# Two staging cycles instead of one, in the first pair of blocks that two phases share

## The chip, the cores and the metric

One Trainium2 chip, one core. The metric is the device time of one execution, in microseconds (us). Engines: TensorE (PE, matrix products), VectorE (DVE), ScalarE (ACT), GpSimd (POOL, nearly idle here) and SyncE (SP, which issues almost all transfers, in order).

## The reference

```python
qn = q / (norm(q, axis=1) + 1e-6);  kn = k / (norm(k, axis=1) + 1e-6)   # over 6016 tokens
a = softmax(kn.T @ qn / tau)                   # 256 x 256
x = v @ a                                      # 6016 x 256
h = relu(x @ w_in);   x = (h * h) @ w_out      # 2048 wide
xn = x / sqrt(mean(x * x) + 1e-6) * rms_g
out = (silu(xn @ w_gate) * (xn @ w_val)) @ w_out2   # 1536 wide
```

All is float32. The kernel splits each operand into a high and a low part and makes three products of one.

## The kernel before

The 6016 tokens are twelve blocks (ten of 512, two of 448). The attention matrix is folded into `w_in`, so the first layer is one product with `m_h`/`m_l`. Blocks 0 to 3 take the plain way (`mlp1`). From pair `FIRST = 2` on (blocks 4 and 5) two blocks go through together (`mlp1_pair`): seven products of combined operands take the place of eight. A pair has eight groups; a group is seven products (21 matmuls, L1415) and four times six matmuls of the second product (L110 to L112, `acc`). The second layer (`mlp2`, L1547) comes after all pairs.

Besides its own work, a pair carries two queues of small steps for ACT and DVE, taken one step of each at three places of every group (`aside`):

- `side`: the norm of the results of the pair before, and then `pair_steps`, which forms that pair's seven operands x0, x4, x6, x3, x1, x2, x5 for the second layer. `hi(i)` casts the high part into a staging tile on ACT (L1099) and stores it (L1102); `lo(i)` makes the low part on DVE (L1110) and stores it (L1111), one step later.
- `tokens`: `v_steps`, which forms the seven v operands of the next pair in the same manner (ACT L1279, DVE L1287, one store at L1342), in the order v0, v4, v3, v1, v2, v6, v5.

All engines take their instructions in the order in which this code is written. The rows of instructions below are in that order.

In pair `FIRST` both queues draw their tiles from one cycle, `first_stage`: tile `ys`, tile `p6`, tile `ys` (the pool has two `ys` tiles), in turn, whoever asks. So that two steps do not ask at once, `aside` stops after one that stages (`staged`). In the pairs after it, the pair operands have two tiles of their own:

```python
first_stage = staged(*["ys", "p6", "ys"] * 4, "ys", "ys")
...
stage = first_stage if first else staged("ys", "p2", "ys") if last else kept(2)
```

`kept(2)` takes two `ys` tiles once and hands them out in turn. At the end of a pair, SP fetches the next pair's v operands (L1162, L1364) and loads the raw v blocks of the pair after that (L464), which DVE transposes (L1266).

Of the kernel before, what the change touches and what calls it, by code (L numbers as in the profile page):

```python
# [11 lines left out]
F32R = mybir.dt.float32r  # L12
# [8 lines left out]
P = 128  # L21
NB = 512
# [6 lines left out]
def attn_moe_kernel(ctx: ExitStack, tc, q, k, v, tau, w_in, w_out, w_gate, w_val, w2, rms_g, out):  # L29
# [16 lines left out]
    q, k, v = q[0], k[0], v[0]  # L46
# [9 lines left out]
    FIRST = NP - 4  # L56

    ctx.enter_context(tc.manual_schedule())
    wp = ctx.enter_context(tc.tile_pool(name="wp", bufs=1))
# [4 lines left out]
    def f32(t):  # L64
        return t.bitcast(F32)
# [7 lines left out]
    def acc(i):  # L73
        return ps.tile([P, NB], F32, tag=f"acc{i}", name=f"acc{i}", bufs=2)
# [44 lines left out]
    NC7 = 7  # L119
# [349 lines left out]
    def place(k, dt=F32R):  # L469
        pool = vp if k < 2 else xp  # L470
        return pool.tile([P, 2, NB], dt, tag=f"p{k}", name=f"p{k}")
# [581 lines left out]
    def staged(*tags):  # L1053

        turns = cycle(tags)

        def tile():
            t = next(turns)
            if t[0] == "p":
                return place(int(t[1]))  # L1060
            pool, k = (xp, 2) if t == "ys" else (vp, 1)
            return pool.tile([P, 2, NB], F32R, tag=t, name="xp", bufs=k)

        return tile

    def kept(count):

        turn, ts = cycle(range(count)), []

        def tile():  # L1070
            if not ts:
                ts.extend(xp.tile([P, 2, NB], F32R, tag="ys", name="xp", bufs=2) for _ in range(count))
            return ts[next(turn)]

        return tile

    def only(e, f):
        def g():
            f()

        g.only = e
        return g
# [253 lines left out]
    def through_dram(p, tile):  # L1336

        def into(i, n):
            if p not in v_dram:
                v_dram[p] = dp.tile([P, NC7, 2, NB], F32, tag=f"v{p}", name="vd")  # L1340
            t = tile()[:, :, :n]
            return t[:, 0], t[:, 1], lambda: nc.sync.dma_start(out=v_dram[p][:, i, :, :n], in_=f32(t))  # L1342

        return into
# [21 lines left out]
    def mlp1_pair(p, ops, side, after_product, after_group):  # L1366


        n = blocks[2 * p][1]
        o = {}  # L1370
        G = NF1 // 2
        if not pw:
            pw.extend(place(k, F32) for k in (3, 4, 5))
        rx, ry, sq = (x[:, :, :n] for x in pw)
        left = []

        def down(f, t, d, ph, pl, first, last):
            def g():
                if first:
                    o[t, d] = acc(d)[:, :n]  # L1380
                ds = slice(d * P, (d + 1) * P)
                mm3(o[t, d], wo_h[:, f, ds], wo_l[:, f, ds], ph, pl, first, last)
                if last:
                    nc.scalar.copy(out=pair_state(p)[:, SLOT[t][d], :n], in_=o[t, d])
                    summed[p] = summed.get(p, 0) + 1

            return g

        def square(r, q, f, t, first, last, lag):

            st = {}

            def hi():
                w = work()[:, :, :n]
                st["h"], st["l"] = w[:, 0], w[:, 1]
                nc.scalar.activation(out=st["h"], in_=r, func=AF.Square)  # L1396

            def full(act):
                if act:
                    nc.scalar.activation(out=q, in_=r, func=AF.Square)  # L1400
                else:
                    nc.vector.tensor_tensor(out=q, in0=r, in1=r, op=ALU.mult)  # L1402

            def lo():
                nc.vector.tensor_tensor(out=st["l"], in0=q, in1=f32(st["h"]), op=ALU.subtract)  # L1405
                due = slots["n"] + lag
                waiting.extend((due, down(f, t, d, st["h"], st["l"], first, last)) for d in range(KC))

            return hi, full, lo

        def group(g):
            def product(i, a, bank, start):
                xh, xl = ops[i]
                for j, (w, x) in enumerate(((0, xh), (1, xh), (0, xl))):
                    nc.tensor.matmul(bank, m_part(a, w, g), x, start=start and j == 0, stop=j == 2,  # L1415
                                     skip_group_check=not start)
                after_product(g, i)

            def aside(k=1):
                staged = False  # L1420
                for q in [side] * k + [tokens]:
                    if q and not getattr(q[0], "takes_bank", False):
                        if p == FIRST and staged and getattr(q[0], "staged", False):
                            break
                        f = q.pop(0)
                        if f is None:
                            continue
                        staged = getattr(f, "staged", False)
                        x = f()
                        if x:  # L1430
                            x()

            turn3 = slots["g"] % 3
            slots["g"] += 1
            b0, *b = [mm()[:, :n] for _ in range(4)]
            bh, bu, bv = b[turn3:] + b[:turn3]
            f0, f1, first, last = 2 * g, 2 * g + 1, g == 0, g == G - 1
            cp, sums = nc.scalar.copy, nc.vector._custom_dve
            product(0, A11, b0, True)
            old = left.pop() if left else leftover.pop() if leftover else None  # L1440
            cp(out=bu, in_=b0)
            if old:
                old[0]()
                old[1](False)
                old[2]()
            down_slot()
            product(3, S1, bh, True)
            aside()
            down_slot()
            product(1, S2, bu, False)  # L1450
            uw = work(F32)[:, :, :n]
            u, w = uw[:, 0], uw[:, 1]
            cp(out=bv, in_=bu)
            cp(out=u, in_=bu)
            down_slot()
            product(4, A12, b0, False)
            nc.scalar.activation(out=rx[:, 0], in_=b0, func=AF.Relu)  # L1457
            hi, full, lo = square(rx[:, 0], sq[:, 0], f0, 0, first, False, 3)
            hi()
            full(False)  # L1460
            lo()
            down_slot()
            product(2, S3, bv, False)
            cp(out=w, in_=bv)
            sums(TENSOR_ADD_SAT, out=rx[:, 1], in0=bh, in1=w, s0=FMAX, s1=0.0)  # L1465
            down_slot()
            down_slot()
            if side and getattr(side[0], "takes_bank", False):
                side.pop(0)(b0)()
            aside()  # L1470
            hi, full, lo = square(rx[:, 1], sq[:, 1], f1, 1, first, False, 2)
            hi()
            full(g % 2 == 0)
            lo()
            product(5, A22, bv, False)
            nc.scalar.activation(out=ry[:, 0], in_=bv, func=AF.Relu)
            hi, full, lo = square(ry[:, 0], sq[:, 0], f1, 0, False, last, 3)
            hi()
            full(True)
            down_slot()  # L1480
            product(6, S4, bh, False)
            r, q = ry[:, 1], sq[:, 1]
            if p == NP - 1 and last:
                x = work(F32)[:, :, :n]
                r, q = x[:, 0], x[:, 1]
            sums(TENSOR_ADD_SAT, out=r, in0=bh, in1=u, s0=FMAX, s1=0.0)
            lo()
            aside(1 + (p > FIRST and g == 1))
            down_slot()
            left.append(square(r, q, f0, 1, False, last, 4))  # L1490
            after_group(g)

        for g in range(G):
            group(g)
        leftover.append(left.pop())
# [278 lines left out]
    ys = {b: parts[b][2] for b in (0, 1)}  # L1774
# [147 lines left out]
    side, tokens = [], []  # L1922
    side.extend(kept_steps)
    drained.append(lambda: (side.insert(0, n0[0]), side.extend(n1 + pair_steps(FIRST - 1, first_stage))))
    first_stage = staged(*["ys", "p6", "ys"] * 4, "ys", "ys")
    for p in range(FIRST, NP):
        nxt = {}
        last = p == NP - 1
# [1 line left out]
        stage = first_stage if first else staged("ys", "p2", "ys") if last else kept(2)  # L1930
        if last:
            last_chunk["gb"] = only("dve", seq(last_chunk["va"], last_chunk["gb"]))
            last_chunk["vb"] = only("dve", seq(last_chunk["gc"], last_chunk["vb"]))
            tokens += [last_chunk.get(x) for x in LAST_CHUNK]
            side += [bridge.h, bridge.l]
        elif first:
            tokens += v_steps(p + 1, through_dram(p + 1, stage))
        else:
            tokens += wide_steps
        if p + 2 < NP:  # L1940
# [206 lines left out]
```

## Time and profile before

| | |
|---|---|
| median of 3 runs | 1116.4 us (1115.68 to 1116.91) |
| the profiled execution: time, span | 1116.82 us, 1115.0 us |
| PE busy | 1097.9 us, 98% |
| PE weight load busy | 923.7 us, 83% |
| DVE busy, ACT busy | 828.1 us (74%), 787.8 us (71%) |
| mean granted TensorE clock | 0.997 |

PE is busy nearly everywhere; of 40 slices of the span only two are below 90% (70% each): the one from 306.6 to 334.5 us and the last. Matmuls overlap, so the busy share says little of pace; the pace is read from the starts of matmuls.

### The profile page before, as it was taken

How to read it: one execution, taken by the hardware profiler on the slowest of the kernel's cores; microseconds unless marked ns; L12 is line 12 of the kernel's file. 1: busy time of each engine (PE TensorE's matmuls, PEld its weight loads, DVE VectorE, ACT ScalarE, POOL GpSimd, SP SyncE). 2: the span in 40 equal slices, each digit the busy share in tenths (PEclk: the TensorE clock that was granted, in tenths of full speed). 3: DMA queues.
4: the chain of work that ended last, by engine and by line, in shares of the span. 5: the costliest groups of instructions: out<-in, count | busy, mean ns of one | idle time of the engine just before them, and what ended most of it. 6: DMA issues, size and time to landing. Idle time of an engine off the chain costs nothing.

```text
span 1115.0 us, 14668 instructions
## 1 busy us (share of the span) xinstructions
PE 1097.9 (98%) x5122; PEld 923.7 (83%) x5122; DVE 828.1 (74%) x1305; ACT 787.8 (71%) x1441; POOL 57.8 (5%) x72
## 2 busy tenths in 40 slices
PE   9999999999979999999999999999999999999997
PEld 8978888888757888889988888888888888888997
DVE  7988888778857987988958888777556666665655
ACT  8788888787657777778777777776665556555554
POOL 2621101000000000000000000000000000000000
PEclk9999999999999999999999999999999999999999
DMA  9642222221344263271276666204423241404001
GB/s 347 211 113 96 76 57 86 71 100 57 123 170 123 94 242 92 104 259 60 87 267 254 211 222 203 97 9 164 132 76 133 76 133 45 156 20 123 19 20 34
DMA packets 115818, 138.33 MB, mean 124 GB/s; under 512 B 52000, under 2 KB 73504, under 8 KB 115616
## 3 DMA queue, kind: packets, MB, share of 16 engines
q1 hardware_dynamic: 113472, 136.54, 36.5%
q10 hardware_dynamic: 2272, 0.85, 0.3%
q8 instruction: 40, 0.66, 0.2%
q14 instruction: 34, 0.28, 0.1%
HBM read 91.10 MB, written 46.27 MB: 123 GB/s over the span
## 4 chain that ended last, share of the span: by engine, by line
PE 69%; DMA 1%; DVE 0%; SPq 0%; issue 0%; ACT 0%; DVEq 0%
PE mm L1547 30%; PE mm L1415 10%; PE acc L111 10%; PE acc L112 10%; PE acc L110 10%; DMA p<-in_v_dram 1%; PE acc L1679 0%; SPq L464 0%; SPq L1364 0%; SPq L1162 0%; DVE sh L1405 0%; DVE vx L1266 0%; DVE xp L1110 0%; DVE ot L1693 0%; DVE hp L1636 0%
## 5 line engine op out<-in xcount | busy, mean ns | idle before, releaser
L1547 PE MATMUL mm<-p,gv 128*128 128x512 f32 (+1 forms) x1188 | 301.9, 387 | 0.0
L1547 PEld LDWEIGHTS mm<-p,gv 128*128 128x128 f32 x1188 | 222.0, 188 | 44.8 <-DVE hp L1627 1.0
L1652 DVE TENSOR_TENSOR sh<-hp,sh 128x512 fp32r<-128x512 f32 (+1 forms) x144 | 97.9, 680 | 111.1 <-ACT sh L1648 110.0
L1602 ACT COPY mm<-mm 128x512 f32<-128x512 f32 (+1 forms) x72 | 40.4, 562 | 157.8 <-PE mm L1547 152.0
L111 PE MATMUL acc<-sh,wo_h 128*128 128x512 f32 (+1 forms) x384 | 149.1, 388 | 1.8 <-DVE sh L1405 1.8
L110 PE MATMUL acc<-sh,wo_h 128*128 128x512 f32 (+1 forms) x384 | 148.9, 388 | 2.0 <-ACT sh L1396 2.0
L112 PE MATMUL acc<-sh,wo_l 128*128 128x512 f32 (+1 forms) x384 | 148.6, 387 | 0.0
L110 PE MATMUL acc<-sh,w_h 128*128 128x512 f32 (+1 forms) x284 | 109.5, 386 | 0.0
L112 PE MATMUL acc<-sh,w_l 128*128 128x512 f32 (+1 forms) x284 | 109.5, 385 | 0.0
L111 PE MATMUL acc<-sh,w_h 128*128 128x512 f32 (+1 forms) x284 | 109.5, 385 | 0.0
L1405 DVE TENSOR_TENSOR sh<-p,sh 128x512 fp32r<-128x512 f32 (+1 forms) x127 | 85.8, 676 | 28.0 <-ACT p L1400 12.5
L1648 ACT CAST sh<-hp 128x512 fp32r<-128x512 f32 (+1 forms) x144 | 89.0, 618 | 2.8 <-DVE hp L1636 1.9
L1396 ACT ACTIVATE sh<-p 128x512 fp32r<-128x512 f32 (+1 forms) x127 | 78.6, 619 | 11.5 <-DVE p L1465 8.4
L111 PEld LDWEIGHTS acc<-sh,wo_h 128*128 128x128 f32 x384 | 72.2, 188 | 16.8 <-DVE sh L1405 3.3
L110 PEld LDWEIGHTS acc<-sh,wo_h 128*128 128x128 f32 x384 | 72.3, 188 | 16.2 <-ACT sh L1396 2.8
L112 PEld LDWEIGHTS acc<-sh,wo_l 128*128 128x128 f32 x384 | 72.4, 188 | 13.8 <-DVE wo_l L182 0.3
L1547 PE MATMUL mm<-xs,gv 128*128 128x512 f32 (+1 forms) x324 | 82.6, 381 | 0.0
L1402 DVE TENSOR_TENSOR p<-p 128x512 f32<-128x512 f32 (+1 forms) x79 | 53.3, 674 | 32.7 <-ACT p L1457 32.6
L1636 DVE TENSOR_TENSOR hp<-mm,sg 128x512 f32<-128x512 f32 (+1 forms) x72 | 48.8, 678 | 34.3 <-PE mm L1547 33.6
L1627 DVE TENSOR_TENSOR hp<-mm,pu 128x512 f32<-128x512 f32 (+1 forms) x72 | 49.0, 680 | 28.1 <-ACT pu L1626 28.0
L1547 PEld LDWEIGHTS mm<-xs,gv 128*128 128x128 f32 x324 | 60.8, 188 | 10.2
L881 DVE TENSOR_TENSOR sh<-p,sh 128x512 fp32r<-128x512 f32 x64 | 45.2, 706 | 27.5 <-ACT sh L874 25.3
(286 smaller groups left out, 2200.2 us busy)
## 6 DMA issues: line engine op xcount, KB each, us to landing
p<-xd SPq DMA_DIRECT2D x102, 256.0 KB, 4.3
xd<-xp SPq DMA_DIRECT2D x62, 256.0 KB, 2.0
xs<-xd SPq DMA_DIRECT2D x12, 512.0 KB, 5.7
out_dram<-ot SPq DMA_DIRECT2D x40, 128.0 KB, 2.3
qraw<-in_q_dram SPq DMA_DIRECT2D x13, 384.0 KB, 7.2
qraw<-in_k_dram SPq DMA_DIRECT2D x13, 384.0 KB, 7.5
raw<-in_moe_w_out_dram SPq DMA_DIRECT2D x9, 512.0 KB, 3.5
vd<-p SPq DMA_DIRECT2D x9, 512.0 KB, 2.6
```

The costliest lines, as they stand in the source:

```text
L110: nc.tensor.matmul(o, wh, xh, start=start, stop=False)
L111: nc.tensor.matmul(o, wh, xl, start=False, stop=False)
L112: nc.tensor.matmul(o, wl, xh, start=False, stop=stop)
L1396: nc.scalar.activation(out=st["h"], in_=r, func=AF.Square)
L1402: nc.vector.tensor_tensor(out=q, in0=r, in1=r, op=ALU.mult)
L1405: nc.vector.tensor_tensor(out=st["l"], in0=q, in1=f32(st["h"]), op=ALU.subtract)
L1415: nc.tensor.matmul(bank, m_part(a, w, g), x, start=start and j == 0, stop=j == 2, skip_group_check=not start)
L1547: nc.tensor.matmul(bank, c[:, hl, a, fs], x, start=start and j == 0, stop=j == 2, skip_group_check=not start)
L1627: add(out=h22, in0=bh, in1=w, op=ALU.add)
L1636: dve(out=h21, in0=bv, in1=sg1, op=ALU.mult)
L1648: nc.scalar.copy(out=parts[t][0], in_=x)
L1652: dve(out=pl, in0=x, in1=f32(ph), op=ALU.subtract)
```

## The change

The pair operands of pair `FIRST` are staged in `kept(2)`, as in the pairs after it. The v operands are staged in three thirds of one tile with the tag `gv0`, which nothing else holds at that time. The rule of one staged step at a time goes. Tile `p6` stages nothing any more.

```diff
+    def slots3(tag):
+
+        turn, ts = cycle(range(3)), []
+
+        def tile():
+            if not ts:
+                ts.append(wp.tile([P, NC7, NB], F32R, tag=tag, name="st"))
+            k = 2 * next(turn)
+            return ts[0][:, k : k + 2]
+
+        return tile
+
...
             def aside(k=1):
-                staged = False
                 for q in [side] * k + [tokens]:
                     if q and not getattr(q[0], "takes_bank", False):
-                        if p == FIRST and staged and getattr(q[0], "staged", False):
-                            break
                         f = q.pop(0)
                         if f is None:
                             continue
-                        staged = getattr(f, "staged", False)
                         x = f()
...
-    first_stage = staged(*["ys", "p6", "ys"] * 4, "ys", "ys")
+    first_stage = kept(2)
...
-            tokens += v_steps(p + 1, through_dram(p + 1, stage))
+            tokens += v_steps(p + 1, through_dram(p + 1, slots3("gv0")))
```

PE and POOL have the same instructions in the same order; ACT and DVE have the same number, SP too. Later lines move: L1099 becomes L1111, L1110 L1122, L1279 L1291, L1287 L1299, L1402 L1414, L1405 L1417.

The first place is ACT from the second half of group 4 of pair `FIRST` (counted from 0) to the first places of group 5, where the casts of the pair operands begin. `xst` is the result of the pair before, `xp` a `ys` tile, `p_2888` tile `p6`; DMAHW with a number counts the landings of one transfer in eight. Before:

```order
L1464 COPY sh<-mm 128x512 [waits PE_49]
L1099 CAST xp<-xst 128x512 [waits DMAHW1_49]
L1396 ACTIVATE sh<-p_2444 128x512 [waits DVE_49]
L1400 ACTIVATE p_2446<-p_2444 128x512
L1476 ACTIVATE p_2445<-mm 128x512 [waits PE_49]
L1396 ACTIVATE sh<-p_2445 128x512 [waits Activation_49]
L1400 ACTIVATE p_2446<-p_2445 128x512
L1099 CAST p_2888<-xst 128x512 [waits DMAHW2_49]
L1441 COPY mm<-mm 128x512 [waits PE_49]
L1396 ACTIVATE sh<-p_2445 128x512 [waits DVE_49]
L1099 CAST xp<-xst 128x512 [waits DMAHW4_49,DMAHW3_49,DVE_49]
```

and now:

```order
L1472 COPY sh<-mm 128x512 [waits PE_49]
L1111 CAST xp<-xst 128x512 [waits DMAHW3_49,DMAHW2_49]
L1291 CAST st<-vt 128x512 [waits DMAHW1_49]
L1408 ACTIVATE sh<-p_2444 128x512 [waits DVE_49]
L1412 ACTIVATE p_2446<-p_2444 128x512
L1484 ACTIVATE p_2445<-mm 128x512 [waits PE_49]
L1408 ACTIVATE sh<-p_2445 128x512 [waits Activation_49]
L1412 ACTIVATE p_2446<-p_2445 128x512
L1111 CAST xp<-xst 128x512 [waits DMAHW5_49,DMAHW4_49]
L1449 COPY mm<-mm 128x512 [waits PE_49]
L1408 ACTIVATE sh<-p_2445 128x512 [waits DVE_49]
L1111 CAST xp<-xst 128x512 [waits DMAHW3_49,DVE_49]
```

The v5 cast (`st<-vt`) has moved from the end of group 6 to this place, and the third cast, x6, which waited for both stores of x0 (DMAHW3 and 4 before), now waits for the store of the high part of x0 alone (DMAHW3 now).

The second place is DVE at the same time; `xst<-xst` forms an operand, ISA is the relu of a sum, L1405 (now L1417) makes the low part that PE's second product waits for. Before:

```order
L1465 ISA p_2444<-mm,sh 128x512 [waits Activation_49]
L1092 TENSOR_TENSOR xst<-xst 128x512
L1405 TENSOR_TENSOR sh<-p_2446,sh 128x512 [waits PE_49,Activation_49]
L1486 ISA p_2445<-mm,sh 128x512 [waits PE_49]
L1405 TENSOR_TENSOR sh<-p_2446,sh 128x512 [waits Activation_49]
L1110 TENSOR_TENSOR xp<-xst,xp 128x512 [waits DMAHW1_49]
L1092 TENSOR_TENSOR xst<-xst 128x512 [waits DVE_49]
L1402 TENSOR_TENSOR p_2446<-p_2445 128x512 [waits DVE_49]
```

and now:

```order
L1473 ISA p_2444<-mm,sh 128x512 [waits Activation_49]
L1104 TENSOR_TENSOR xst<-xst 128x512
L1299 TENSOR_TENSOR st<-p_2643,st 128x512 [waits DMAHW0_49]
L1417 TENSOR_TENSOR sh<-p_2446,sh 128x512 [waits PE_49,Activation_49]
L1494 ISA p_2445<-mm,sh 128x512 [waits PE_49]
L1417 TENSOR_TENSOR sh<-p_2446,sh 128x512 [waits Activation_49]
L1122 TENSOR_TENSOR xp<-xst,xp 128x512
L1104 TENSOR_TENSOR xst<-xst 128x512 [waits DVE_49]
L1299 TENSOR_TENSOR st<-vt,st 128x512 [waits DMAHW1_49]
L1414 TENSOR_TENSOR p_2446<-p_2445 128x512 [waits DVE_49]
```

The low parts of v6 and v5 (L1299) have moved here from the end of group 6 and the start of group 7.

The third place is SP at the end of pair `FIRST`: the last two stores of a pair operand, and then the fetches for the next pair (`p_3076`, `vf`, `vr`). Before:

```order
L1102 DMA xd<-xp 128x512
L1111 DMA xd<-xp 128x512
L1342 DMA vd<-xp 128x1024
L1162 DMA p_3076<-vd 128x512 x2
L1162 DMA vf<-vd 128x512 x4
L1342 DMA vd<-xp 128x1024
L1162 DMA vr<-vd 128x512 x6
L1364 DMA vd<-vd 128x512 x2
L464 DMA p_3170<-in_v_dram 32x16x64 x4
L464 DMA vx<-in_v_dram 32x16x64 x4
```

and now:

```order
L1114 DMA xd<-xp 128x512
L1123 DMA xd<-xp 128x512
L1174 DMA p_3067<-vd 128x512 x2
L1174 DMA vf<-vd 128x512 x4
L1174 DMA vr<-vd 128x512 x6
L1376 DMA vd<-vd 128x512 x2
L464 DMA p_3159<-in_v_dram 32x16x64 x4
L464 DMA vx<-in_v_dram 32x16x64 x4
```

The stores of v6 and v5 no longer stand between the fetches.

## Rows read from the trace of the kernel before

**Rows 1.** Timeline of PE, the last product of seven groups: start, length, instruction

```profile
302.40 0.39 PE L1415 MATMUL mm<-vd,ch 128*128 128x512 f32 x1
...
315.27 0.39 PE L1415 MATMUL mm<-vd,ch 128*128 128x512 f32 x1
...
333.18 0.39 PE L1415 MATMUL mm<-vd,ch 128*128 128x512 f32 x1
...
343.40 0.39 PE L1415 MATMUL mm<-vd,ch 128*128 128x512 f32 x1
...
354.41 0.39 PE L1415 MATMUL mm<-vd,ch 128*128 128x512 f32 x1
...
405.72 0.39 PE L1415 MATMUL mm<-vd,ch 128*128 128x512 f32 x1
...
415.92 0.39 PE L1415 MATMUL mm<-vd,ch 128*128 128x512 f32 x1
```

**Rows 2.** Waits of PE from 302 to 331 us: total, times, longest

```profile
PE mm L1415 <- ACT mm L1441: 3.3, 1, 3.3
PE acc L110 <- ACT sh L1396: 2.0, 2, 1.1
PE acc L111 <- DVE sh L1405: 1.0, 2, 0.8
PE mm L1415 <- ACT mm L1453: 0.5, 1, 0.5
```

**Rows 3.** Stretches: length, busy PE, PEld, DVE, ACT, POOL, PEclk, DMA share, GB/s

```profile
290.80:301.00 10.20, 10.20 (x46) 8.45 (x46) 8.03 (x14) 7.64 (x14) 0.00 (x0) 1.00 0.34 130
326.00:330.00 4.00, 4.00 (x13) 3.08 (x12) 1.75 (x3) 2.29 (x4) 0.00 (x0) 0.57 0.61 196
362.00:372.00 10.00, 10.00 (x47) 8.27 (x46) 9.58 (x16) 7.06 (x14) 0.00 (x0) 1.00 0.13 52
```

**Rows 4.** Timelines of DVE and PE in group 4 of the pair

```profile
292.25 0.69 DVE L1405 TENSOR_TENSOR sh<-p,sh 128x512 fp32r<-128x512 f32 x1 [0.62 <-ACT p L1400]
...
284.13 0.50 PE L111 MATMUL acc<-sh,wo_h 128*128 128x512 f32 x1 [0.35 <-DVE sh L1405]
...
294.47 0.39 PE L111 MATMUL acc<-sh,wo_h 128*128 128x512 f32 x1
```

**Rows 5.** Waits of ACT from 292 to 331 us

```profile
ACT xp L1099 <- DMA xd<-xp: 7.3, 2, 3.7
ACT xp L1279 <- DVE p L1402: 3.4, 1, 3.4
ACT xp L1099 <- DVE p L1110: 1.9, 1, 1.9
ACT xp L1099 <- DVE sh L1405: 1.8, 1, 1.8
```

**Rows 6.** Timeline of ACT, casts of x3 and v5, idle before in brackets

```profile
304.24 0.62 ACT L1099 CAST xp<-xst 128x512 fp32r<-128x512 f32 x1 [3.65 <-DMA xd<-xp]
...
324.14 0.62 ACT L1279 CAST xp<-vt 128x512 fp32r<-128x512 f32 x1 [3.41 <-DVE p L1402]
```

**Rows 7.** Timeline of SP, stores of the low parts of x6 and x5

```profile
302.20 0.32 SPq L1111 DMA_DIRECT2D xd<-xp  x1
...
322.08 0.32 SPq L1111 DMA_DIRECT2D xd<-xp  x1
```

**Rows 8.** Groups of ACT by line, next pair, 376 to 406 us; idle before last

```profile
L1099 ACT CAST xp<-xst 128x512 fp32r<-128x512 f32 x7 | 4.3, 610 | 0.0
```

**Rows 9.** Timelines of SP and DVE at the start of the next pairs

```profile
336.98 2.80 SPq L464 DMA_DIRECT2D p<-in_v_dram  x4
...
417.29 2.96 SPq L464 DMA_DIRECT2D p<-in_v_dram  x4
...
344.37 1.31 DVE L1266 STREAM_TRANSPOSE vx<-p 128x512 f32<-128x512 f32 x2 [1.82 <-DMA p<-in_v_dram]
```

**Rows 10.** Transfers by issue: count, KB each, median us to landing

```profile
vd<-p SPq DMA_DIRECT2D x9, 512.0 KB, 2.6
```

## The prediction

> **What bounds the kernel now.** I read the page's slices first: PE is full everywhere but in one slice near 307 to 334 us, the end of pair `FIRST`, and at the very end. What is to be won is what PE loses there. The busy share does not measure it, since matmuls overlap, so I took the start of one fixed matmul of each group, the first of its last product, `vd,ch` [rows 1]. Undisturbed, two groups follow each other by 415.92 − 405.72 = 10.20 us. From group 5 to group 6 of pair `FIRST` it takes 315.27 − 302.40 = 12.87, from 6 to 7 333.18 − 315.27 = 17.91, and the next two steps, into the next pair, take 10.22 and 11.01. Over the clean pace that is 2.67 + 7.71 = **10.38 us lost in two steps**, and 0.81 in the first group of the next pair.
>
> What PE waits for in that stretch [rows 2]: 3.3 + 2.0 + 1.0 + 0.5 = 6.8 us in six waits, all of it for ACT's and DVE's ordinary work for the pair (copies of a bank, parts of the hidden layer), which comes late. The granted clock from 326 to 330 us is 0.57 [rows 3], between its two levels of 1.2 and 2.4 GHz; it fell behind the longest wait, 3.3 us. That is 4.0 × (1 − 0.57) = 1.7 us of full-speed work not done. The remaining 10.38 − 6.8 − 1.7 = 1.9 us are the restarts: the first matmul behind a wait takes 0.50 us instead of 0.39 [rows 4], and the next ones follow at a wider distance.
>
> Why ACT is late: it waits 7.3 + 3.4 + 1.9 + 1.8 = 14.4 us, in five casts into staging tiles [rows 5]. The releaser named there differs, the distance to a store does not. x3's cast starts at 304.24, and the store of the low part of x6 was issued at 302.20; v5's cast starts at 324.14, and that of x5 was issued at 322.08 [rows 6, 7]. The distances are 2.04 and 2.06 us, and the three other casts lie 2.05 to 2.08 behind the store before them. So each of these casts takes a tile whose store has just been issued, and waits until it has landed. The instructions say the same: x6's cast names both stores of x0. One of the two `ys` tiles is out of the turn: v6 was cast into it in group 4, and its low part is made only at the end of group 6, since the rule of one staged step lets `side` go first. What should be a cycle of three is one `ys` tile and `p6`, and whenever that `ys` tile comes up twice running, the wait stands in ACT's queue ahead of all that PE needs.
>
> **The change, part by part.**
>
> *Two tiles for the pair operands.* A step now takes the tile of two steps back. Steps are a third of a group apart, 10.20 / 3 = 3.4 us; the high half is stored right behind its cast, lands some 2.06 us after the issue [rows 6, 7], and is asked for again two steps on, 6.8 us after its cast. The next pair stages its seven casts so already, and ACT is idle 0.0 us ahead of them [rows 8]. So the five waits go, 14.4 us on ACT, and with them PE's 10.38: the waits (6.8), the restarts (1.9), and the clock, which has no long wait left to fall behind (1.7). The other end is that part of the waits comes back; at 10.38 / 14.4 = 0.72 us of PE per us of ACT's waiting, each us costs 0.7.
>
> *Three thirds for the v operands.* A third is asked for again three steps on, its store is issued one step on; that leaves two steps, 6.8 us, for a landing of 2.6 [rows 10]. Nothing.
>
> *The rule goes: v6 and v5 move into group 4.* That puts one cast on ACT (0.62 us [rows 6]) and two subtractions on DVE (0.69 each, as L1405 in [rows 4]) into a stretch of 10.20 us in which DVE is busy 8.03 and ACT 7.64 [rows 3]: 9.4 and 8.3. In the next pair DVE does 9.58 in 10.00 while PE is full [rows 3]. What queues behind them on DVE is L1405, the low part that PE's second product waits for. The one right behind v6's subtraction waits 0.62 us for ACT as it is, starts at 292.25 and is done at 292.94; PE takes its result at 294.47 [rows 4]: 1.53 us of room, of which ACT's extra cast uses some 0.6. So the cost is nothing, by that cover. Without it, one late part costs what the wait of this kind at 284.13 does, 0.35 us idle [rows 4], about 0.7 with the restart. That wait stands ahead of everything that moves, and stays. Groups 6 and 7 are rid of the same work.
>
> *SP at the end of the pair.* The fetches no longer queue behind the stores of v6 and v5. The raw v loads were issued at 336.98, 3.80 behind the last product of group 7; one pair later it is 417.29 − 415.92 = 1.37 [rows 1, 9]. If pair `FIRST` comes to the same, they start 2.4 us sooner against PE, and DVE's first transpose, which waited 1.82 us for them [rows 9], does not wait; behind it on DVE stands the low part for which PE then waits, and that is the 0.81 us in the first group. The bounds are 0 and 0.81; I take 0.8, since 2.4 is more than 1.82.
>
> Sum: 10.38 + 0.8 = **11.2 us**. The profiled execution took 1116.82 (a span of 1115.0, and 1.8 around it): 1105.6. It lies 0.4 above the median of the runs, 1116.4, from which the same sum gives **1105.2 us**.
>
> One term of it rests on a single execution: the clock's 1.7 us [rows 3]. Without that term the sum is 9.5 and the time 1106.9. The Trainium skill, "TensorE: Matmul & The Clock Gate", section "Part 1: The HAM clock gate (the "warmup" mystery)", speaks against counting on it: the monitor that grants the clock runs freely, so where the clock changes, and how many matmuls are slow, varies from run to run of one kernel. No row here shows such a variation; the three runs lie within 1.2 us.
>
> **The rivals.**
>
> 1. *New lateness on ACT and DVE.* Two steps at one place push a low part beyond its room in groups 4 to 6. For it: PE waited for DVE in just this way at 284.13 [rows 4]. Against: the 1.53 us of room, and the next pair, as full and without loss. Price, once in each of three groups, 3 × 0.7 = 2.1: 1107.3.
> 2. *The clock's share is not in the timed runs*, because there the long wait does not bring the clock down: 1106.9, as above.
> 3. *The change does not do what it says*: the casts wait for DVE, as three of the five waits name it [rows 5], and not for stores; then they stay, and the time is 1116. Against: the five equal distances behind a store, and that the other two name one.
> 4. *Slower: the thirds are held as one tile*, so that each v cast waits for the store of the v operand just before it. Six casts would wait as the x casts do, 14.4 / 5 = 2.9 us, and 2.6 − 2.06 = 0.5 more for the larger transfer [rows 5, 10]: 20 us on ACT, in groups 2 to 5, at 0.72 some 14.7 on PE, against 11.2 won: 1119.9. It decides once five of the six wait so: 5 × 3.4 × 0.72 = 12.2 us, more than is won. Against: v casts name one landing each, that of three steps back, and the third of them none, while the second's store is young.
>
> **How the numbers follow.** Forecast 0.80; rival 1 0.08, rival 2 0.06, rival 3 0.03, rival 4 0.03. The predicted time is that of the forecast, 1105.2. The range goes down to 1104.4 (the 0.7 us at 284.13 gone as well) and up to 1108.0, which takes in rivals 1 and 2 and a returned us of waiting (0.7); 0.94 by the cases. A measurement of this kernel can tell 0.2%, 2.2 us, from no change: the forecast and rivals 1 and 2 are faster by more, 0.94, rival 3 is the same, 0.03, rival 4 slower, 0.03.
>
> **What would show it.** In the profile after, the seven x casts of pair `FIRST` have no idle time ahead of them; the `vd,ch` matmuls of its groups 4 to 7 follow each other by 10.2; the clock stays at 1.00; the slice of 70% is gone. The raw v loads are issued about 1.4 us behind the last product of group 7, and the transposes do not wait. The prediction is wrong if a cast into `st` or `xp` still waits for a store, if L1417 turns up among the releasers of PE in groups 4 to 6, or if the time won there comes back as a wait in the next pair.

## The result and the profile after

The changed kernel takes 1105.36 us (median of 4 runs, 1105.12 to 1106.24) against 1116.34 of the kernel before: ratio 0.9903, 95% interval 0.9886 to 0.992. The profiled execution took 1105.12, its span is 1103.3.

The slices of the page, PE, in tenths, before and then after: the slice of 70% in the middle is gone.

```profile
PE   9999999999979999999999999999999999999997
```

```profile
PE   9999999999999999999999999999999999999997
```

The timeline of PE, the same matmul as in [rows 1], groups 5, 6 and 7 of pair `FIRST` and groups 0 and 1 of the next pair:

```profile
301.92 0.39 PE L1427 MATMUL mm<-vd,ch 128*128 128x512 f32 x1
...
312.12 0.39 PE L1427 MATMUL mm<-vd,ch 128*128 128x512 f32 x1
...
322.31 0.39 PE L1427 MATMUL mm<-vd,ch 128*128 128x512 f32 x1
...
332.54 0.39 PE L1427 MATMUL mm<-vd,ch 128*128 128x512 f32 x1
...
342.74 0.39 PE L1427 MATMUL mm<-vd,ch 128*128 128x512 f32 x1
```

The steps are 10.20, 10.19, 10.23 and 10.20 where they were 12.87, 17.91, 10.22 and 11.01: 52.01 has become 40.82, **11.19 us less**. This is nearly all of the gain: the span is 11.7 us shorter, and the other 0.5 us lies ahead of the pair, where its group 0 comes at 249.60 instead of 250.13. ACT's groups from 280 to 325 us say why (the last number is the idle time ahead):

```profile
L1111 ACT CAST xp<-xst 128x512 fp32r<-128x512 f32 x7 | 4.3, 616 | 0.0
```

Four of these seven casts waited before, 11.0 us in all, and v5's cast 3.4; now none of them waits. Of PE's waits from 240 to 345 us one is left, and it is the old one of [rows 4], ahead of everything that moved:

```profile
PE acc L111 <- DVE sh L1417: 0.4, 1, 0.4
```

Two stretches, as in [rows 3]: the first now holds v6's and v5's steps, the second is all that was disturbed before.

```profile
290.80:301.00 10.20, 10.20 (x46) 8.45 (x45) 9.55 (x16) 8.40 (x17) 0.00 (x0) 1.00 0.59 231
...
302.00:345.00 43.00, 43.00 (x191) 35.53 (x190) 30.26 (x47) 33.57 (x61) 0.00 (x0) 1.00 0.55 178
```

DVE goes from 8.03 to 9.55 and ACT from 7.64 to 8.40, PE stays full, and the clock is 1.00 throughout. At the start of the next pair (SP, then DVE) the match is less good:

```profile
324.33 0.95 SPq L464 DMA_DIRECT2D p<-in_v_dram  x2
```

```profile
332.09 1.31 DVE L1278 STREAM_TRANSPOSE vx<-p 128x512 f32<-128x512 f32 x2 [0.40 <-DMA p<-in_v_dram]
```

The raw loads are issued 324.33 − 322.31 = 2.0 us behind the last product, not 1.4, and DVE still waits 0.40 us for them, where it was 1.82 [rows 9]. PE no longer notices.

### The profile page after: what moved, and what is told of

Read it like the earlier page. It is cut to its first block, busy times and chain, and to the rows that moved or that the text cites. A ratio compares the mean times of both kernels' runs of the same rounds, so it can differ in the third digit from the quotient of the medians.

```text
span 1103.3 us, 14660 instructions
## 1 busy us (share of the span) xinstructions
PE 1093.5 (99%) x5122; PEld 922.8 (84%) x5122; DVE 828.5 (75%) x1305; ACT 788.3 (71%) x1441; POOL 38.8 (4%) x72
## 4 chain that ended last, share of the span: by engine, by line
PE 95%; DVE 3%; ACT 1%; DMA 0%; issue 0%; DVEq 0%; ACTq 0%
PE mm L1555 31%; PE acc L111 13%; PE acc L112 13%; PE acc L110 13%; PE mm L1427 12%; PE mm L112 3%; PE mm L110 2%; PE mm L111 2%; PE mm L662 1%; PE acc L671 1%; PE acc L670 1%; PE acc L672 1%; PE mm L795 1%; DVE sh L1417 0%; DMA qraw<-in_k_dram 0%; DVE p L1414 0%
## 5 line engine op out<-in xcount | busy, mean ns | idle before, releaser
L1417 DVE TENSOR_TENSOR sh<-p,sh 128x512 fp32r<-128x512 f32 (+1 forms) x127 | 85.8, 676 | 19.8 <-ACT p L1412 7.9
L1414 DVE TENSOR_TENSOR p<-p 128x512 f32<-128x512 f32 (+1 forms) x79 | 53.3, 675 | 31.8 <-ACT p L1465 31.6
```

## The experiments

The theory: ACT waited for the landing of stores, because one `ys` tile was held by v6 and the other came up twice running. The change has two parts that could each end this, the tiles and the rule.

**The tiles change, the rule stays.** To the changed kernel:

```diff
+                        if p == FIRST and staged and getattr(q[0], "staged", False):
+                            break
```

> The changed kernel with its tiles (two for the pair operands, three thirds for the v operands), but with the rule of before: no second staged step at one place. v6's low part and v5 stay at the end of group 6 and the start of group 7. Theory (ACT waited for stores of a tile taken again at once): the seven casts of the pair operands have no idle ahead of them, PE keeps 10.2 us a group, and of the 11.2 us only the 0.8 of the next pair's first group is lost again, because the stores of v6 and v5 stand between SP's fetches: 1106.2 us. Rival (it is the rule that makes the steps late, not the tiles): ACT waits as before and the time is 1116.

Measured: 1107.92 us (1107.16 to 1108.49), ratio 0.9927 (0.9912 to 0.9942), span 1105.4. ACT's seven casts are idle 0.0 us ahead, and the steps in the pair are 10.20 to 10.22: the tiles alone end the waits, so the rival falls. But more is lost in the next pair than I had said, 344.55 − 332.56 = 11.99, which is 1.8 over the clean pace (PE):

```profile
332.56 0.39 PE L1427 MATMUL mm<-vd,ch 128*128 128x512 f32 x1
...
344.55 0.39 PE L1427 MATMUL mm<-vd,ch 128*128 128x512 f32 x1
```

SP and DVE of the same kernel show the way there:

```profile
319.72 1.60 SPq L1354 DMA_DIRECT2D vd<-st  x1
321.43 5.13 SPq L1174 DMA_DIRECT2D vr<-vd  x6
...
327.55 0.43 SPq L464 DMA_DIRECT2D p<-in_v_dram  x1
```

```profile
334.53 1.30 DVE L1278 STREAM_TRANSPOSE vx<-p 128x512 f32<-128x512 f32 x2 [2.82 <-DMA p<-in_v_dram]
```

The store of v5 stands ahead of the fetches, the raw loads come 327.55 − 322.34 = 5.2 us behind the last product of group 7, and DVE waits 2.82 us. In the kernel before the loads came 3.80 us behind it; there PE's own waits came between.

**The rule goes, the tiles stay.** To the kernel before:

```diff
-                        if p == FIRST and staged and getattr(q[0], "staged", False):
-                            break
```

> The kernel before without its rule, with the one cycle of three tiles for both queues. Theory in its narrow form (the cycle of three became one of two only because the rule kept v6 in a ys tile from group 4 to group 6): v6's tile is back after one step, each step takes a tile that was stored some steps before, ACT's casts wait 1 us or less in all, the v steps are out of SP's way too, and the time is 1105.4 to 1106.5, with no tiles added at all. Rival (three tiles for two queues are too few, since two steps at one place now use two of them): the casts still wait about 2 us behind a store, at least four of them, and the time is 1112 to 1116.

Measured: 1105.89 us (1105.76 to 1106.20), ratio 0.991 (0.9893 to 0.9926), span 1104.0. The groups of ACT from 245 to 345 us:

```profile
L1099 ACT CAST xp<-xst 128x512 fp32r<-128x512 f32 x6 | 3.7, 617 | 1.8 <-DVE xp L1110 1.4 <-DMA xd<-xp 0.4
...
L1279 ACT CAST p<-vt 128x512 fp32r<-128x512 f32 x2 | 1.2, 615 | 0.5 <-DMA vd<-p 0.5
L1279 ACT CAST p<-vx 128x512 fp32r<-128x512 f32 x2 | 1.2, 610 | 0.0
L1099 ACT CAST p<-xst 128x512 fp32r<-128x512 f32 x1 | 0.6, 624 | 0.0
```

2.3 us of waits are left of 14.4, more than the 1 us that I had given them, with the old cycle of three tiles. What shortened the cycle was the rule, which kept v6 in its tile. The waits that are left cost PE 0.76 us idle once, in one step of 302.47 − 291.23 = 11.24, which is 1.0 over the clean pace. This one step is all that the tiles of the change add in the trace; by time, 1105.89 and 1105.36 cannot be told apart.

**One tile for the pair operands.** To the changed kernel:

```diff
-    first_stage = kept(2)
+    first_stage = staged("p6")
```

> The changed kernel, but the pair operands are staged in one tile (p6), taken anew for each, so that each of six casts takes the tile of the step just before it. Theory (a cast into a tile whose low part was just stored waits until that has landed, about 2.05 us behind the issue, at about 2.9 us of ACT's waiting each, and PE loses 0.72 us for each): 17 to 20 us of waits on ACT, 12 to 15 us on PE, 1117.5 to 1120.5 us; the clock falls again where a wait on PE is over 3 us. Rival (the casts wait for DVE, which makes the low part before, and not for the landing): 0.7 us each on ACT, 4 us in all, about 1108 us.

Measured: 1122.81 us (1121.94 to 1123.43), ratio 1.006 (1.0045 to 1.0075). ACT's casts:

```profile
L1111 ACT CAST p<-xst 128x512 fp32r<-128x512 f32 x7 | 4.3, 618 | 21.1 <-DMA xd<-p 17.4 <-issue 3.6
```

Six waits of 3.4 to 3.7 us, 21.1 in all, each ending 2.04 to 2.12 us behind the issue of the store of the step before: the mechanism, made at will. One of them, the store on SP and the cast on ACT:

```profile
301.10 0.32 SPq L1123 DMA_DIRECT2D xd<-p  x1
```

```profile
303.22 0.62 ACT L1111 CAST p<-xst 128x512 fp32r<-128x512 f32 x1 [3.48 <-DMA xd<-p]
```

Over the clean pace, the three steps from group 4 to group 7 are 6.48 + 6.54 + 2.42 = 15.4 us longer, which is 0.73 per us of ACT's waiting, where the kernel before had 0.72. The first step of the next pair is 1.6 longer as well: SP issues the last store at 333.05, and the raw loads come 343.62 − 338.87 = 4.75 us behind the last product of group 7. That I had left out, and the waits were each 0.6 us longer than the mean that I took, so the time lies above what was expected. The rival, waits for DVE alone, falls.

**One tile for the v operands.** To the changed kernel:

```diff
-            if not ts:
-                ts.append(wp.tile([P, NC7, NB], F32R, tag=tag, name="st"))
-            k = 2 * next(turn)
-            return ts[0][:, k : k + 2]
+            return wp.tile([P, 2, NB], F32R, tag=tag, name="st")
```

> The changed kernel, but the v operands are staged in one tile, taken anew for each, so that each v cast waits for the store of the v operand before it. This is rival 4 of the prediction, made on purpose. By its price: 3.4 us on ACT for each of six casts, 20 us, and at 0.72 some 14.7 us on PE: about 1120 us. Rival (v steps lie further apart than the pair's, a store has landed before the next cast for most of them): only v1 and v5, cast at the place of the low part before, wait, 5 to 7 us on ACT, 1108 to 1111 us.

Measured: 1124.80 us (1124.67 to 1125.87), ratio 1.0081 (1.0066 to 1.0096). Five of ACT's casts wait 2.0 to 6.4 us each for `vd<-st`:

```profile
L1288 ACT CAST st<-p 128x512 fp32r<-128x512 f32 x4 | 2.5, 615 | 13.2 <-DMA vd<-st 13.2
L1288 ACT CAST st<-vt 128x512 fp32r<-128x512 f32 x3 | 1.8, 614 | 9.3 <-DMA vd<-st 9.3
```

22.5 us on ACT (20 were expected, from six casts) cost four steps 4.7 + 5.8 + 5.0 + 4.4 = 19.9 us against the changed kernel, 0.88 per us. So rival 4 of the prediction would have made the kernel slower by more than I priced; the change does not meet it, since the thirds of its tile are held apart.

**POOL issues the stores of the v operands**, to the kernel in which the rule stays:

```diff
-            return t[:, 0], t[:, 1], lambda: nc.sync.dma_start(out=v_dram[p][:, i, :, :n], in_=f32(t))
+            eng = nc.gpsimd if p == FIRST + 1 else nc.sync
+            return t[:, 0], t[:, 1], lambda: eng.dma_start(out=v_dram[p][:, i, :, :n], in_=f32(t))
```

> The kernel of the run in which the tiles change and the rule stays, with the stores of the v operands issued by POOL in place of SP, so that SP's fetches for the next pair and the raw v loads stand behind no store. In that run the raw loads were issued 5.2 us behind the last product of group 7 and the first step of the next pair took 11.99 us. Theory (the late v6 and v5 cost through their place in SP's queue): the raw loads are issued 2 to 3 us behind, and the step falls to 10.2 to 10.6. Rival (v5's late low part itself keeps its source tile and the fetches that need it): the loads stay 4 us or more behind, the step at 11.5 or more. Times: 1106 by the theory, 1107.5 or more by the rival; POOL's own way of issuing may add a landing time that no run has shown.

Measured: 1107.15 us (1107.00 to 1108.84), ratio 0.9918 (0.9904 to 0.9933). SP:

```profile
317.78 2.22 SPq L1174 DMA_DIRECT2D vf<-vd  x4
320.16 5.16 SPq L1174 DMA_DIRECT2D vr<-vd  x6
325.61 1.05 SPq L1377 DMA_DIRECT2D vd<-vd  x2
326.80 0.33 SPq L464 DMA_DIRECT2D p<-in_v_dram  x1
```

The raw loads come 326.80 − 322.27 = 4.5 us behind the last product instead of 5.2, and the step is 343.80 − 332.49 = 11.31 instead of 11.99. So 0.7 of the 1.8 us goes when the stores leave SP's queue, and 1.1 stays. The rival puts that on v5's late low part, which keeps the fetches late, whoever issues its store. But POOL's stores also land later:

```profile
vd<-st POOLq DMA_DIRECT2D x7, 512.0 KB, 3.0
```

That is 0.4 us more than SP's 2.6 [rows 10], so how the 1.1 is shared between v5's lateness and POOL's way of issuing is not shown. The outcome lies between the two numbers, nearer to the rival's.

**One place later for v1, v2, v6 and v5.** To the changed kernel, behind the line that fills `tokens` in pair `FIRST`:

```diff
+            tokens.insert(10, None)
```

> The changed kernel with one empty turn ahead of the low part of v1 in the queue of v steps of the first shared pair, so that v1's low part, v2, v6 and v5 come one place later. The one wait that is left on PE in that pair, 0.36 us idle at 283.63 (0.75 us by the pace of the groups), comes from a low part of the hidden layer that stands on DVE behind the norm's transpose and v1's subtraction. Theory: with v1's subtraction behind it the low part is done 0.6 us sooner, the step from group 3 to group 4 falls from 10.98 to about 10.3, nothing new is late in groups 4 and 5, and the time is 0.7 us less than the changed kernel's, 1104.7. Rival (DVE is behind by more than one subtraction since group 2, and the work moved makes groups 4 and 5 late): the step stays over 10.7 or a later one grows by as much, 1105.4 or more.

Measured: 1104.59 us (1104.23 to 1105.37), ratio 0.9891 (0.9874 to 0.9907). PE:

```profile
281.41 0.48 PE L1427 MATMUL mm<-vd,ch 128*128 128x512 f32 x1
...
291.76 0.39 PE L1427 MATMUL mm<-vd,ch 128*128 128x512 f32 x1
```

The step from group 3 to group 4 is 10.35 (10.98 in the changed kernel), no later one grows, and PE waits for nothing in the pair (one cast of the pair operands now waits 0.5 us for DVE, at no cost to PE). In the profiles the stretch from group 0 of the pair to group 1 of the next is 92.50 us long against 93.14. The profiled executions as a whole do not show it: the span is 1103.6 against 1103.3, since group 0 of the pair came 0.69 us later. It has the lowest median here and is clearly faster than the kernel before; that it is faster than the changed kernel the times do not show.

## Why the prediction was right

*The size of the loss* (10.38 us in two steps, 0.8 in the next pair): right. The two steps from group 5 to group 7 went from 30.78 to 20.39 us, 10.39 less, and the first step of the next pair from 11.01 to 10.20.

*Why ACT is late*: shown from both sides. When no tile comes up twice running the waits go (all with the tiles alone, all but 2.3 of 14.4 us with the rule alone gone); with a tile that comes up at each step they are there at each step, at the same 2.04 to 2.12 us behind a store. The prediction named v6, parked by the rule, as the reason, and the run without the rule bears it out. It did not see that the two parts are each almost enough: the tiles alone give 8.3 us, the rule alone 10.3, both 11.0 (differences of the medians, each against its own runs of the kernel before).

*The exchange rate*: 0.72 us of PE for one of ACT held for casts of the pair operands (0.73), but not for the v casts (0.88). The two traces show where the difference lies. These are the stretches from group 4 to group 7 with one tile for the pair operands, and from group 1 to group 5 with one tile for the v operands (length, busy PE, PEld, DVE, ACT, POOL, PEclk, DMA share, GB/s):

```profile
292.80:338.90 46.10, 35.68 (x137) 26.66 (x136) 24.18 (x39) 22.77 (x42) 0.00 (x0) 0.93 0.30 112
```

```profile
259.70:321.40 61.70, 49.40 (x183) 38.17 (x182) 39.91 (x65) 33.15 (x61) 0.15 (x1) 0.89 0.20 81
```

PE is idle 10.4 and 12.3 us, 0.49 and 0.55 per us of ACT's waiting. The lower clock costs, counted as in the prediction, 46.10 × (1 − 0.93) = 3.2 and 61.70 × (1 − 0.89) = 6.8 us, which is 0.15 and 0.30. So the greater part of the difference is the clock, which fell twice in the one run and four times in the other.

*v6 and v5 in group 4 at no cost*: right. DVE rose by 1.5 and ACT by 0.8 us (1.4 and 0.6 forecast), and PE stayed full.

*The clock's 1.7 us*: right in size as far as it can be told. The profile after holds 1.00 through the stretch. The medians fell by 11.0, which is nearer to 11.2 than to 9.5, and all four runs lie below the 1106.9 of rival 2; but the interval of the ratio, 8.9 to 12.7 us, holds both, so rival 2 is unlikely and not excluded. The mean granted clock of the timed runs points the same way: 0.994 to 0.998 in the fourteen runs of the kernel before that ran beside the experiments, 0.998 and 0.999 in the four of the changed kernel. By the rule of the Trainium skill, "TensorE: Matmul & The Clock Gate", section "Part 1: The HAM clock gate (the "warmup" mystery)", slow matmuls vary in number from run to run. The spread of the mean clock is in line with that, but the time does not follow it run by run: the kernel before took 1116.90 us once at 0.994 and once at 0.998.

*SP at the end of the pair* (0.8 us): the number was right, its way only in part. I put it on the stores of v6 and v5 in SP's queue. The two runs with the rule show that the place in the queue is 0.7 of 1.8 us there; the rest stays when another engine issues the stores. What all runs agree on is the lateness of the raw loads: at 1.6 to 2.0 us behind the last product (four kernels) the first step of the next pair loses nothing, at 3.8, 4.5, 4.75 and 5.2 us it loses 0.81, 1.11, 1.58 and 1.79 us. After the change they came at 2.0 us, not 1.4, so that the transposes still wait 0.40 us; PE has that much room.

## What to carry to other kernels

A cycle of n tiles is only as long as the number of tiles that are free in it: one user who keeps a tile for long makes the others take the same tile twice running, and then each waits for a landing on an engine that has other work behind it. Equal distances between a store's issue and the start of the stalled instruction show this, where the releaser named in the profile differs from row to row. And a rule that holds back work, to spare tiles, can hold back the very step that would free one: try the kernel without the rule before adding tiles.

## What the runs showed of the hardware

The clock fell behind shorter waits than I had taken for needed. With one tile for the pair operands PE waited 2.17 us at 299.24 and 2.12 at 304.38, and was busy between; the clock is at full speed up to 305 and 0.57 on average from 305 to 309 us, as behind the 3.3 us wait of the kernel before:

```profile
299.24 0.50 PE L1427 MATMUL mm<-vx,ch 128*128 128x512 f32 x1 [2.17 <-ACT mm L1449]
304.38 0.96 PE L1427 MATMUL mm<-vr,c 128*128 128x512 f32 x3 [2.12 <-ACT mm L1461]
```

```profile
299.00:305.00 6.00, 3.64 (x15) 2.71 (x16) 1.90 (x3) 2.52 (x6) 0.00 (x0) 1.00 0.49 195
305.00:309.00 4.00, 4.00 (x12) 3.13 (x11) 3.53 (x6) 1.44 (x3) 0.00 (x0) 0.57 0.12 45
```

In the same run it fell a second time behind a wait of 3.38 us (0.62 on average from 318 to 322), as I had expected there. With one tile for the v operands it fell even behind waits of 1.43 and 0.75 us, though it had been back at 1.00 since 306 us:

```profile
310.48 0.49 PE L110 MATMUL acc<-sh,wo_h 128*128 128x512 f32 x1 [1.43 <-ACT sh L1405]
311.73 0.50 PE L111 MATMUL acc<-sh,wo_h 128*128 128x512 f32 x1 [0.75 <-DVE sh L1414]
```

```profile
310.00:312.00 2.00, 0.77 (x2) 0.46 (x3) 1.02 (x2) 1.97 (x5) 0.00 (x0) 1.00 0.00 0
312.00:314.00 2.00, 2.00 (x7) 1.58 (x7) 1.63 (x4) 2.00 (x5) 0.00 (x0) 0.67 0.00 0
```

So in the prediction "no long wait left to fall behind" was the wrong measure, though nothing depended on it here, as no wait is left in the two steps.

A store of 256 KB from SP is landed, and ACT released, 2.04 to 2.12 us behind its issue in all eleven waits (five in the kernel before, six with one tile for the pair operands). Twice the size takes longer: with one tile for the v operands, the casts that wait for a store of 512 KB start 2.64 to 2.67 us behind its issue in four cases and 3.30 in a fifth. The medians from issue to landing in the kernel before say the same, 2.0 for 256 KB and 2.6 for 512 KB [rows 10]:

```profile
xd<-xp SPq DMA_DIRECT2D x62, 256.0 KB, 2.0
```

If the time is a fixed part and a part by size, an estimate from these numbers is 0.6 us for each 256 KB and 1.4 to 1.5 us fixed. The Trainium skill, "DMA: Bandwidth & Descriptors", section "Anatomy of one DMA — SWDGE (gpsimd) path", has for stores that GpSimd issues a fixed cost of about 2.0 us, most of it the receipt of the last byte, and bytes by a rate of 436 GB/s, which is 0.6 us for 256 KB (an estimate). The part by size agrees with SP's stores here; the fixed part is smaller by about half a microsecond. For the 512 KB that POOL issued, the same page gives 3.2 us (an estimate), and 3.0 was measured.
